# Attention: row sums by a column of ones, high halves on ScalarE, the sinks' values on GpSimd

## The chip, the cores and the metric

The kernel runs on one core of a Trainium2 chip. The metric is the device time of one execution in microseconds (us). A core has TensorE (matmuls, results in PSUM), VectorE, ScalarE, GpSimd, and SyncE, which here only issues transfers. Each engine runs its own instructions in its own order and waits on semaphores for the others.

## The reference

Three stages. Attention over batch 4, 8 heads, 768 positions, head width 64, with a window of 128 keys and 4 sink keys that every query sees; then a mixture of experts (top 1 of 8) over 3072 tokens; then a dense layer with x - tanh(x). The change is in the first stage alone, which computes

```
scores = scale * np.matmul(q, k.transpose(0, 1, 3, 2))
keep = is_sink | in_window                      # pos < n_sink, 0 <= rel < window
scores = np.where(keep, scores, -1000000000.0)
a = np.exp(scores - np.max(scores, axis=-1, keepdims=True))
a = a / (np.sum(a, axis=-1, keepdims=True) + 1e-09)
return np.matmul(a, v).astype(np.float32)
```

## The kernel before

Float32 operands are split into two float16 halves (high, and low = value - high), and a product is made of three matmuls: high x high, high x low, low x high.

*Units and slots.* Attention goes by units: a unit is a pair of heads of one batch, 16 in all. A unit has 6 query blocks of 128 positions (index i), each with two heads (h). The loop of stage_a runs over slots (102 of them); in a slot each step works on another block, with lags (LAG): scores of block s, mask and row maximum of s-1, exponentials of s-2, transposes and high halves of s-3, low halves of s-4, values of s-6. The engines' queues get the instructions in this written order, slot by slot:

```
ORDER = ["tr", "exp0", "exp1", "high", "low", "mask", "sc", "val"]
```

and at the end of each slot what was put down for it with later(), in the order in which it was put down, then the preparation of the next unit's values (prep_steps), then at_slot, which in the late slots loads and halves the first experts' weights (w.load on SyncE, w.prep on ScalarE and VectorE).

*Steps of a block.* mask_max (VectorE, L238) reads scores from PSUM, adds the mask and gives the row extreme; exps (ScalarE, L246) gives the exponentials and, by an accumulator that a second instruction reads, their row sums (sums); transposes (TensorE, L260); high (ScalarE, L266); low (VectorE, L272); values (TensorE, L283 to L285), which accumulates outputs in two PSUM banks, oa for blocks 0 to 3 and ob for 4 and 5.

*Sinks.* The weights of the 4 sink keys of the blocks that don't hold them in their window are gathered three times over into 48 columns (sink_weights), transposed after the values of blocks 2 and 4 (sink_turn), and split on VectorE: L296 casts the transposed weights to float16, L297 subtracts them where the low half is wanted. L288 multiplies them with VSK, the sinks' values. VSK comes from step vs of prep_steps: two VectorE instructions (L195 cast, L196 low half where wanted) and a GpSimd product with a block mask (L198).

*Normalization.* divisors (GpSimd, L302) adds 1e-9 to the sums, reciprocals (VectorE, L307), normal (VectorE, L317) multiplies the PSUM outputs with them: part 0 of 512 columns in the slot of block 4's values, part 1 of 256 columns in a later one. halves then splits the result in three parts of two blocks, on GpSimd (L181 high, L182 low). Ahead of each, SyncE issues a transfer (L327) that moves data only if a general path had been taken; it is not, but the instruction stands in SyncE's queue and its semaphore is waited for. turn (L339, L340 on SyncE) transposes the halves by DMA for the routing and copies them into token rows; SyncE's queue also holds the loads of q, k, v, of zeros and of weights. In the tail the last unit's halves are split by ScalarE (L330) and VectorE (L331).

Of the kernel before, what the change touches and what calls it, by code (L numbers as in the profile page):

```python
# [10 lines left out]
F32 = mybir.dt.float32  # L11
# [173 lines left out]
def prep_steps(nc, e, u):  # L185

    def v(h):
        if h == 0:
            u.V = e.tp.tile([128, 2, 2, NB, 64], F16, tag="V", name="V", bufs=3)
        f = lambda t: t.rearrange("p t d -> p (t d)")  # L190
        split2(nc, f(u.V[:, 0, h]), f(u.V[:, 1, h]), u.vf[:, S // 2 * h:S // 2 * h + S // 2])

    def vs():
        s16 = e.tp.tile([48, 64], F16, tag="s16", name="s16", bufs=2)
        nc.vector.tensor_copy(s16, u.sf)  # L195
        nc.vector.scalar_tensor_tensor(s16, s16, e.vlow, u.sf, op0=ALU.mult, op1=ALU.add)  # L196
        u.VSK = e.tp.tile([48, 4, 64], F16, tag="VSK", name="VSK", bufs=3)
        nc.gpsimd.tensor_tensor(u.VSK, s16.unsqueeze(1).to_broadcast([48, 4, 64]),  # L198
                                e.bmask.unsqueeze(2).to_broadcast([48, 4, 64]), op=ALU.mult)
    return [lambda: v(0), lambda: v(1), vs]  # L200
# [11 lines left out]
def scores(nc, e, u, i):  # L212

    if i == 0:
        u.mn, u.sums, u.rs = (e.sm.tile([128, 12], F32, tag=t, name=t, bufs=3) for t in ("mn", "sums", "rs"))
    if i % 2 == 0:
        u.P[i // 2] = e.pp.tile([128, 4, 2 * BR], F32, tag="P", name="P")
    c0 = c_first(i)
    n = 264 - c0
    k0 = max(i - 1, 0) * BR + (c0 if i else 4)  # L220
    kc, qc = slice(k0, k0 + n), slice(128 * i, 128 * i + 128)
    u.s[i] = []

# [51 lines left out]
def values(nc, e, u, i):  # L275
    if i in (0, 4):
        u.o.append(bank(e, ("oa", "ob")[i // 4]).rearrange("p (n d) -> p n d", d=64))
    p = u.PT.pop(i)
    bs = blocks(i)
    for j, (h, t) in enumerate(bs):  # L280
        o = u.o[i // 4][:, (2 * i + h) % 8]
        vh, vl = u.V[:, 0, h, t], u.V[:, 1, h, t]
        nc.tensor.matmul(o, lhsT=p[:, 0, j], rhs=vh, start=j == 0 and i in (0, 4), stop=False, skip_group_check=True)  # L283
        nc.tensor.matmul(o, lhsT=p[:, 0, j], rhs=vl, start=False, stop=False, skip_group_check=True)
        nc.tensor.matmul(o, lhsT=p[:, 1, j], rhs=vh, start=False, stop=False, skip_group_check=True)  # L285
    if i in (3, 5):
        o = u.o[0][:, 4:8] if i == 3 else u.o[1][:, 0:4]
        nc.tensor.matmul(o, lhsT=u.pks[i // 2 - 1], rhs=u.VSK, start=False, stop=True, skip_group_check=True)  # L288


def sink_turn(nc, e, u, part):
# [4 lines left out]
    nc.vector.tensor_copy(t, pk)  # L296
# [3 lines left out]
def divisors(nc, e, u, part):  # L300
    s = slice(*((0, 8), (8, 12))[part])
    nc.gpsimd.tensor_scalar(u.rs[:, s], u.sums[:, s], 1e-9, 1.0 / XS, op0=ALU.add, op1=ALU.mult)  # L302


def reciprocals(nc, e, u, part):
    s = slice(*((0, 8), (8, 12))[part])
    nc.vector.reciprocal(u.rs[:, s], u.rs[:, s])  # L307
# [12 lines left out]
def halves(nc, e, u, part, fast=False):  # L320

    a, z = ((0, 2), (2, 4), (4, 6))[part]
# [4 lines left out]
    nc.sync.dma_start(x[:, a:z], e.xg[r:r + 256, :].rearrange("(t p) c -> p t c", p=128), cond=e.genr, cond_hint=False)  # L327
# [198 lines left out]
def stage_a(tc, e, us, at_slot):  # L526

    nc = tc.nc
    with tc.tile_pool(name="tp", bufs=2) as e.tp, tc.tile_pool(name="pp", bufs=4) as e.pp, \
         tc.tile_pool(name="pw", bufs=4) as e.pw:  # L530
        units = [(b, hp) for b in range(B) for hp in range(H // 2)]
# [14 lines left out]
        def after(s, u):  # L546
# [10 lines left out]
            later(s + HALF2, lambda: halves(nc, e, u, 2))  # L557
# [16 lines left out]
        for s in range(last + 1):  # L574
# [856 lines left out]
```

## Time and profile before

| | |
|---|---|
| runs | 1053.58, 1054.61, 1057.43 us (median 1054.61) |
| profiled execution, its own time | 1058.27 us |
| its span, first to last instruction | 1056.6 us |
| mean granted TensorE clock | 0.968 of full speed |
| busy: TensorE / VectorE / ScalarE / GpSimd | 980.5 / 549.5 / 430.0 / 307.1 us |
| attention stage | about 14 to 223 us of the span |
| expert and dense stages | from about 223 us to the end |

Busy times are shares of the whole span; in the attention stage VectorE, ScalarE and GpSimd are much busier than later. The matmuls' ends are modelled, so a busy TensorE isn't TensorE at its peak.

### The profile page before, as it was taken

What the parts mean: (1) busy time and instruction counts of PE and PEld (TensorE: products, weight loads), DVE (VectorE), ACT (ScalarE), POOL (GpSimd) and SP (SyncE); (2) the same over time, 40 slices, a digit from 0 to 9 for tenths busy, and PEclk for the clock granted to TensorE, in tenths of its full rate; (3) what the DMA queues carried; (4) which work ended last, traced back from release to release, by engine and by line L of the source; (5) the groups of instructions that cost most, each with busy time, mean ns of one, the idle gap of its engine ahead of it and who ended that gap; (6) DMA issues with size and microseconds to landing.
All of it is one profiled execution on the core that took longest, in us unless ns stands there. A gap on an engine that the chain in (4) does not pass through costs nothing. (4 is left out here: it accounts for less than half of the span.)

```text
span 1056.6 us, 18953 instructions
## 1 busy us (share of the span) xinstructions
PE 980.5 (93%) x6883; PEld 546.3 (52%) x6883; DVE 549.5 (52%) x1283; ACT 430.0 (41%) x1210; POOL 307.1 (29%) x409
## 2 busy tenths in 40 slices
PE   6998987798887899999989999999999999999996
PEld 4665655575556466666644444444444444444442
DVE  5999998956325458473748987251151052053000
ACT  3787877743223344343425552351152152053000
POOL 4657766622000000000005552242142143143010
PEclk6999998799999999999999999999999999999998
DMA  4796789587729768693533316102002000000000
GB/s 139 223 260 198 211 184 289 167 177 239 183 80 221 205 187 249 133 271 92 152 84 80 100 46 175 40 1 60 20 1 50 30 1 11 24 8 10 21 31 21
DMA packets 144944, 123.45 MB, mean 117 GB/s; under 512 B 101488, under 2 KB 113776, under 8 KB 144816
## 3 DMA queue, kind: packets, MB, share of 16 engines
q1 hardware_dynamic: 130608, 85.70, 32.0%
q0 software_dynamic: 8160, 28.34, 8.3%
q10 hardware_dynamic: 6048, 7.76, 2.4%
q8 instruction: 72, 1.18, 0.4%
q14 instruction: 56, 0.46, 0.1%
HBM read 75.97 MB, written 23.79 MB: 94 GB/s over the span
## 5 line engine op out<-in xcount | busy, mean ns | idle before, releaser
L1089 DVE SCALAR_TENSOR_TENSOR w<-z 128x512 f32<-128x512 f32 x96 | 72.6, 756 | 215.1 <-ACT z L1087 211.6
L1077 POOL TENSOR_TENSOR gl<-w,gh 128x512 f16<-128x512 f32 x96 | 117.4, 1223 | 151.2 <-ACT gh L1076 150.9
L660 PE MATMUL s<-y,wi 128*128 128x512 f16 x384 | 145.5, 379 | 0.0
L661 PE MATMUL s<-y,wi 128*128 128x512 f16 x384 | 145.5, 379 | 0.0
L662 PE MATMUL s<-y,wi 128*128 128x512 f16 x384 | 145.5, 379 | 0.0
L660 PE MATMUL pt<-wo,gh 128*128 128x512 f16 x352 | 133.4, 379 | 0.0
L661 PE MATMUL pt<-wo,gh 128*128 128x512 f16 x352 | 133.4, 379 | 0.0
L662 PE MATMUL pt<-wo,gl 128*128 128x512 f16 x352 | 133.4, 379 | 0.0
L1087 ACT ACTIVATE z<-s 128x256 f32<-128x256 f32 x192 | 72.0, 380 | 107.8 <-PE s L662 107.2
L246 ACT ACTIVATE P<-P,mn 128x264 f32<-128x264 f32 (+1 forms) x192 | 93.5, 489 | 36.5 <-DVE mn L238 36.1
L728 POOL DMA_DIRECT2D w<-in_w_dram x30 | 16.2, 540 | 291.8 <-DVE f L741 206.0
L1109 ACT ACTIVATE ot<-pt 128x512 f32<-128x512 f32 x22 | 13.1, 597 | 194.2 <-PE pt L662 184.4
L260 PE MATMUL pt<-ident,P 128*128 128x128 f32 x352 | 62.8, 302 | 23.2 <-DVE PT L272 22.4
L228 PE MATMUL s<-kf,qf 64*128 64x264 f32 (+2 forms) x384 | 76.2, 460 | 7.1 <-DVE mn L238 4.6
L1110 POOL DMA_INDIRECT out_dram<-ot,idu x24 | 23.5, 979 | 195.7 <-ACT ot L1109 186.0
L660 PE MATMUL pt<-w,h 128*128 128x512 f16 x176 | 67.4, 383 | 6.6 <-ACT h L770 3.6
L1090 DVE SCALAR_TENSOR_TENSOR w<-s,w 128x512 f32<-128x512 f32 x96 | 66.4, 692 | 10.4 <-DVE w L1089 0.5
L238 DVE CUSTOM_DVE_ANT_0 P<-s,mask 128x264 f32<-128x264 f32 (+1 forms) x192 | 69.2, 395 | 0.3
L716 DVE SCALAR_TENSOR_TENSOR w<-stg,w 128x1024 f16<-128x1024 f32 x55 | 65.9, 1223 | 6.0 <-ACT w L710 4.1
L662 PE MATMUL pt<-w,h 128*128 128x512 f16 x176 | 67.5, 383 | 1.5 <-issue 1.5
L661 PE MATMUL pt<-w,h 128*128 128x512 f16 x176 | 67.3, 382 | 0.0
L1076 ACT CAST gh<-w 128x512 f16<-128x512 f32 x96 | 59.2, 617 | 11.8 <-DVE w L1090 11.7
(272 smaller groups left out, 2042.9 us busy)
## 6 DMA issues: line engine op xcount, KB each, us to landing
stg<-in_w_dram SPq DMA_DIRECT2D x64, 512.0 KB
w<-in_w_dram POOLq DMA_DIRECT2D x30, 512.0 KB, 4.6
kf<-in_kT_dram SPq DMA_DIRECT2D x16, 396.0 KB
qf<-in_qT_dram SPq DMA_DIRECT2D x16, 384.0 KB
vf<-in_vP_dram SPq DMA_DIRECT2D x16, 384.0 KB
xf<-xg SPq DMA_DIRECT2D x48, 128.0 KB
row<-hl SPq DMA_DIRECT2D x15, 384.0 KB
yc<-y ACTq DMA_DIRECT2D x10, 514.0 KB
```

What stands on the lines that cost most here:

```text
L228: nc.tensor.matmul(ps[:, c0:264], lhsT=u.qf[r, qc], rhs=u.kf[r, kc], start=True, stop=True, skip_group_check=True)
L238: nc.vector.tensor_tensor_reduce(out=u.P[i // 2][:, it % 4, c0:], in0=s[h][:, c0:264], in1=e.M[:, min(i, 2), c0:], op0=ALU.add, op1=ALU.mi ...
L246: nc.scalar.activation(p, p, AF.Exp, scale=-1.0, bias=u.mn[:, it:it + 1], accum_out=u.sums[:, it:it + 1])
L260: nc.tensor.transpose(ps[:, j], u.P[i // 2][:, it % 4, c0:c0 + 128], e.ident)
L660: nc.tensor.matmul(out, lhsT=lh, rhs=rh, start=start, stop=False)
L661: nc.tensor.matmul(out, lhsT=lh, rhs=rl, start=False, stop=False)
L662: nc.tensor.matmul(out, lhsT=ll, rhs=rh, start=False, stop=stop)
L716: nc.vector.scalar_tensor_tensor(lo, src, WS, hi, op0=ALU.mult, op1=ALU.subtract)
L1077: nc.gpsimd.tensor_tensor(gl[:, f], w, gh[:, f], op=ALU.subtract)
L1087: nc.scalar.activation(z[:, s], p[:, s], AF.Square, scale=1.0 / (YS * WIS), accum_out=e.zsum[:, n:n + 1])
L1089: nc.vector.scalar_tensor_tensor(w, z, -2.5, z, op0=ALU.add, op1=ALU.mult)
L1090: nc.vector.scalar_tensor_tensor(w, p, -2.0 / 15.0 * G2 / (YS * WIS), w, op0=ALU.mult, op1=ALU.mult)
```

## The change

Row sums no longer come from ScalarE's accumulator. The high halves of the values get a 65th column of ones (V, in three fixed buffers whose ones are written once), so that the matmuls with the high halves of the values also add the weights up into column 64 of each output block; VSK gets such a column too. Output blocks are 65 columns wide, and oa and ob hold three query blocks each. normal adds 1e-9 to column 64, takes the reciprocal and multiplies, all on VectorE, for three blocks at a time; divisors and reciprocals go. halves has two parts of three blocks; the high half is a ScalarE copy for every unit. In sink_turn the high half is a ScalarE copy too. Step vs is on GpSimd alone (three small instructions and the product with the block mask). The sink matmul of blocks 2 and 3 becomes two, as these lie in different banks.

```diff
 def v(h):
         if h == 0:
-            u.V = e.tp.tile([128, 2, 2, NB, 64], F16, tag="V", name="V", bufs=3)
-        f = lambda t: t.rearrange("p t d -> p (t d)")
-        split2(nc, f(u.V[:, 0, h]), f(u.V[:, 1, h]), u.vf[:, S // 2 * h:S // 2 * h + S // 2])
+            e.V.append(e.V.pop(0))
+            u.V = e.V[0]
+        split2(nc, u.V[:, 0, h, :, 0:64], u.V[:, 1, h, :, 0:64],
+               u.vf[:, S // 2 * h:S // 2 * h + S // 2].rearrange("p (t d) -> p t d", d=64))
 def vs():
-        s16 = e.tp.tile([48, 64], F16, tag="s16", name="s16", bufs=2)
-        nc.vector.tensor_copy(s16, u.sf)
-        nc.vector.scalar_tensor_tensor(s16, s16, e.vlow, u.sf, op0=ALU.mult, op1=ALU.add)
-        u.VSK = e.tp.tile([48, 4, 64], F16, tag="VSK", name="VSK", bufs=3)
-        nc.gpsimd.tensor_tensor(u.VSK, s16.unsqueeze(1).to_broadcast([48, 4, 64]),
-                                e.bmask.unsqueeze(2).to_broadcast([48, 4, 64]), op=ALU.mult)
+        e.s16.append(e.s16.pop(0))
+        s16 = e.s16[0]
+        t = s16[:, 0:64]
+        nc.gpsimd.tensor_scalar(t, u.sf, 1.0, 1.0, op0=ALU.mult, op1=ALU.mult)
+        nc.gpsimd.tensor_tensor(t, t, e.vlow.to_broadcast([48, 64]), op=ALU.mult)
+        nc.gpsimd.tensor_tensor(t, u.sf, t, op=ALU.add)
+        u.VSK = e.tp.tile([48, 4, 65], F16, tag="VSK", name="VSK", bufs=3)
+        nc.gpsimd.tensor_tensor(u.VSK, s16.unsqueeze(1).to_broadcast([48, 4, 65]),
+                                e.bmask.unsqueeze(2).to_broadcast([48, 4, 65]), op=ALU.mult)
 def exps(nc, e, u, i, h):
-    nc.scalar.activation(p, p, AF.Exp, scale=-1.0, bias=u.mn[:, it:it + 1], accum_out=u.sums[:, it:it + 1])
+    nc.scalar.activation(p, p, AF.Exp, scale=-1.0, bias=u.mn[:, it:it + 1])
 def values(nc, e, u, i):
-    if i in (0, 4):
-        u.o.append(bank(e, ("oa", "ob")[i // 4]).rearrange("p (n d) -> p n d", d=64))
+    if i in (0, 3):
+        u.o.append(bank(e, ("oa", "ob")[i // 3])[:, 0:390].rearrange("p (n d) -> p n d", d=65))
...
-        vh, vl = u.V[:, 0, h, t], u.V[:, 1, h, t]
+        vh, vl = u.V[:, 0, h, t], u.V[:, 1, h, t, 0:64]
...
     if i in (3, 5):
-        o = u.o[0][:, 4:8] if i == 3 else u.o[1][:, 0:4]
-        nc.tensor.matmul(o, lhsT=u.pks[i // 2 - 1], rhs=u.VSK, start=False, stop=True, skip_group_check=True)
+        pks = u.pks[i // 2 - 1]
+        for o, v in ((u.o[0][:, 4:6], u.VSK[:, 0:2]), (u.o[1][:, 0:2], u.VSK[:, 2:4])) if i == 3 else \
+                ((u.o[1][:, 2:6], u.VSK),):
+            nc.tensor.matmul(o, lhsT=pks, rhs=v, start=False, stop=True, skip_group_check=True)
 def sink_turn(nc, e, u, part):
-    nc.vector.tensor_copy(t, pk)
+    nc.scalar.copy(t, pk)
     nc.vector.scalar_tensor_tensor(t, t, e.plow, pk, op0=ALU.mult, op1=ALU.add)
-def divisors(nc, e, u, part): ...
-def reciprocals(nc, e, u, part): ...
 def normal(nc, e, u, part):
-    r4 = u.rs[:, s].rearrange("p (i h) -> p i h", h=2).unsqueeze(3).to_broadcast([128, z - a, 2, 64])
-    o = u.o[part][:, 0:2 * (z - a)].rearrange("p (i h) d -> p i h d", h=2)
-    nc.vector.tensor_tensor(u.x[:, a:z], o, r4, op=ALU.mult)
+    o = u.o[part]
+    r = u.rs[:, 6 * part:6 * part + 6]
+    nc.vector.tensor_scalar(r, o[:, :, 64], 1e-9, 1.0 / XS, op0=ALU.add, op1=ALU.mult)
+    nc.vector.reciprocal(r, r)
+    nc.vector.tensor_tensor(u.x[:, 3 * part:3 * part + 3].rearrange("p i h d -> p (i h) d"), o[:, :, 0:64],
+                            r.unsqueeze(2).to_broadcast([128, 6, 64]), op=ALU.mult)
 def halves(nc, e, u, part, fast=False):
-    a, z = ((0, 2), (2, 4), (4, 6))[part]
+    a, z = ((0, 3), (3, 6))[part]
...
-    if fast:
-        nc.scalar.copy(hi, x[:, a:z])
-        (nc.vector if fast else nc.gpsimd).tensor_tensor(lo, x[:, a:z], hi, op=ALU.subtract)
-    else:
-        split2(nc, hi, lo, x[:, a:z])
+    nc.scalar.copy(hi, x[:, a:z])
+    (nc.vector if fast else nc.gpsimd).tensor_tensor(lo, x[:, a:z], hi, op=ALU.subtract)
 def stage_a(tc, e, us, at_slot):
+        e.V = [e.tp.tile([128, 2, 2, NB, 65], F16, name=f"V{i}", bufs=1) for i in range(3)]
+        e.s16 = [e.tp.tile([48, 65], F16, name=f"s16{i}", bufs=1) for i in range(2)]
+        for t in e.V:
+            nc.gpsimd.memset(t[:, 0, :, :, 64:65], 1.0)
+        for t in e.s16:
+            nc.gpsimd.memset(t[:, 64:65], 1.0)
+            nc.gpsimd.memset(t[32:48, 64:65], 0.0)
...
-                            divisors(nc, e, g[0], g[1] // 2 - 1)
...
-                        if i5 in RECIP:
-                            later(s, lambda u=u, p=RECIP.index(i5): reciprocals(nc, e, u, p))
                         if i5 == 3:
                             later(s + 1, lambda u=u: normal(nc, e, u, 0), lambda u=u: halves(nc, e, u, 0))
-                            later(s + HALF1, lambda u=u: halves(nc, e, u, 1))
```

The last part of halves is number 1 now, at the same slot as number 2 before; the tail calls it too.

## Rows read from the trace of the kernel before

**Rows 1.** Busy time of each engine in two stretches of the attention stage.

```profile
core 0: us, PE busy (x) PEld busy (x) DVE busy (x) ACT busy (x) POOL busy (x), PEclk, DMA share, GB/s
...
120.00:132.00 12.00, 11.47 (x147) 7.64 (x146) 11.55 (x46) 10.34 (x38) 8.17 (x16) 1.00 0.66 189
...
204.00:216.00 12.00, 11.09 (x93) 7.18 (x93) 8.55 (x30) 6.45 (x21) 7.75 (x13) 0.57 0.49 134
```

**Rows 2.** Timeline, VectorE, a quiet unit: start, length, line [idle before, releaser].

```profile
118.24 0.41 DVE L317 TENSOR_TENSOR xf<-ob,rs 128x256 f32<-128x256 f32 x1
...
121.55 0.28 DVE L296 CAST pks<-s 48x128 f16<-48x128 f32 x1 [0.15 <-PE s L294]
...
129.00 0.41 DVE L317 TENSOR_TENSOR xf<-ob,rs 128x256 f32<-128x256 f32 x1
```

**Rows 3.** Timeline, VectorE, the slot of block 4 of another unit.

```profile
114.40 0.68 DVE L317 TENSOR_TENSOR xf<-oa,rs 128x512 f32<-128x512 f32 x1
115.00 0.27 DVE L296 CAST pks<-s 48x128 f16<-48x128 f32 x1
115.31 0.34 DVE L297 SCALAR_TENSOR_TENSOR pks<-pks,plow,s 48x128 f16<-48x128 f16 x1
```

**Rows 4.** Groups by form, VectorE, 20 to 400: count | busy us, mean ns | idle.

```profile
L196 DVE SCALAR_TENSOR_TENSOR s<-s,vlow,sf 48x64 f16<-48x64 f16 x14 | 5.9, 418 | 0.5
L195 DVE CAST s<-sf 48x64 f16<-48x64 f32 x14 | 5.6, 400 | 0.0
...
L307 DVE RECIPROCAL rs<-rs 128x8 f32<-128x8 f32 x16 | 3.0, 190 | 0.0
```

**Rows 5.** Timeline, VectorE, a small tensor_scalar behind the stage.

```profile
242.55 0.17 DVE L410 TENSOR_SCALAR gs<-gs 128x6 f32<-128x6 f32 x1
```

**Rows 6.** Groups by form, ScalarE, 20 to 400.

```profile
L246 ACT ACTIVATION_READ_ACCUMULATOR P<-P,mn 128x1 f32 x187 | 35.3, 189 | 0.0
...
L266 ACT CAST PT<-pt 128x256 f16<-128x256 f32 x15 | 5.3, 355 | 1.1 <-PE pt L260 1.1
```

**Rows 7.** Timeline, GpSimd, the cast behind the product of rows 3.

```profile
115.32 0.40 POOL L181 TENSOR_SCALAR hl<-xf 128x256 f16<-128x256 f32 x1 [1.76 <-DVE pks L296]
```

**Rows 8.** Timeline, ScalarE, the last unit's halves in the tail.

```profile
227.40 0.41 ACT L330 CAST hl<-xf 128x256 f16<-128x256 f32 x1 [7.18 <-DMA row<-hl]
```

**Rows 9.** Timeline, TensorE, two successive matmuls of 64 columns.

```profile
115.75 0.19 PE L284 MATMUL ob<-V,PT 128*128 128x64 f16 x1
115.78 0.19 PE L285 MATMUL ob<-V,PT 128*128 128x64 f16 x1
```

**Rows 10.** Timeline, SyncE's queue, the unit at 151.

```profile
153.69 0.42 SPq L327 DMA_DIRECT2D xf<-xg  x2
...
159.07 0.33 SPq L170 DMA_DIRECT2D sf<-in_vS_dram  x1
...
164.35 0.09 SPq L327 DMA_DIRECT2D xf<-xg  x1
```

**Rows 11.** Timeline, VectorE, the two products of that unit.

```profile
151.43 0.67 DVE L317 TENSOR_TENSOR xf<-oa,rs 128x512 f32<-128x512 f32 x1
...
155.43 0.41 DVE L317 TENSOR_TENSOR xf<-ob,rs 128x256 f32<-128x256 f32 x1
```

**Rows 12.** Timeline, ScalarE, at the end of that unit.

```profile
156.41 0.58 ACT L266 CAST PT<-pt 128x512 f16<-128x512 f32 x1
...
160.81 1.06 ACT L710 ACTIVATE w<-stg 128x1024 f16<-128x1024 f32 x1 [1.63 <-DMA stg<-in_w_dram]
```

**Rows 13.** Timeline, SyncE's queue, the tail.

```profile
221.26 2.90 SPq L339 DMA_TRANSPOSE xT<-hl  x1
...
225.18 0.08 SPq L327 DMA_DIRECT2D xf<-xg  x1
```

**Rows 14.** Timeline, VectorE, the last unit's first product.

```profile
221.62 0.69 DVE L317 TENSOR_TENSOR xf<-oa,rs 128x512 f32<-128x512 f32 x1
```

**Rows 15.** Timeline, TensorE, the last sink matmul.

```profile
222.94 0.28 PE L288 MATMUL ob<-VSK,pks 48*128 48x256 f16 x1 [0.86 <-DVE pks L297]
```

More of the change, by code (lines that the diff above doesn't have):

```diff
@@ L214, in scores @@
     if i == 0:
-        u.mn, u.sums, u.rs = (e.sm.tile([128, 12], F32, tag=t, name=t, bufs=3) for t in ("mn", "sums", "rs"))
+        u.mn, u.rs = (e.sm.tile([128, 12], F32, tag=t, name=t, bufs=3) for t in ("mn", "rs"))
     if i % 2 == 0:
@@ L280, in values @@
     for j, (h, t) in enumerate(bs):
-        o = u.o[i // 4][:, (2 * i + h) % 8]
-        vh, vl = u.V[:, 0, h, t], u.V[:, 1, h, t]
-        nc.tensor.matmul(o, lhsT=p[:, 0, j], rhs=vh, start=j == 0 and i in (0, 4), stop=False, skip_group_check=True)
-        nc.tensor.matmul(o, lhsT=p[:, 0, j], rhs=vl, start=False, stop=False, skip_group_check=True)
+        o = u.o[i // 3][:, (2 * i + h) % 6]
+        vh, vl = u.V[:, 0, h, t], u.V[:, 1, h, t, 0:64]
+        nc.tensor.matmul(o, lhsT=p[:, 0, j], rhs=vh, start=j == 0 and i in (0, 3), stop=False, skip_group_check=True)
+        nc.tensor.matmul(o[:, 0:64], lhsT=p[:, 0, j], rhs=vl, start=False, stop=False, skip_group_check=True)
         nc.tensor.matmul(o, lhsT=p[:, 1, j], rhs=vh, start=False, stop=False, skip_group_check=True)
     if i in (3, 5):
-        o = u.o[0][:, 4:8] if i == 3 else u.o[1][:, 0:4]
-        nc.tensor.matmul(o, lhsT=u.pks[i // 2 - 1], rhs=u.VSK, start=False, stop=True, skip_group_check=True)
+        pks = u.pks[i // 2 - 1]
+        for o, v in ((u.o[0][:, 4:6], u.VSK[:, 0:2]), (u.o[1][:, 0:2], u.VSK[:, 2:4])) if i == 3 else \
+                ((u.o[1][:, 2:6], u.VSK),):
+            nc.tensor.matmul(o, lhsT=pks, rhs=v, start=False, stop=True, skip_group_check=True)
 def sink_turn(nc, e, u, part):
@@ L295, in sink_turn @@
     t = u.pks[part] = e.sm.tile([48, 128], F16, tag="pks", name="pks")
-    nc.vector.tensor_copy(t, pk)
+    nc.scalar.copy(t, pk)
     nc.vector.scalar_tensor_tensor(t, t, e.plow, pk, op0=ALU.mult, op1=ALU.add)
[L300 to L307, printed above, removed]
 def normal(nc, e, u, part):
-    a, z = ((0, 4), (4, 6))[part]
     if part == 0:
         u.x = e.rx.tile([128, NB, 2, 64], F32, tag="xf", name="xf")
-    s = slice(2 * a, 2 * z)
-    r4 = u.rs[:, s].rearrange("p (i h) -> p i h", h=2).unsqueeze(3).to_broadcast([128, z - a, 2, 64])
-    o = u.o[part][:, 0:2 * (z - a)].rearrange("p (i h) d -> p i h d", h=2)
-    nc.vector.tensor_tensor(u.x[:, a:z], o, r4, op=ALU.mult)
+    o = u.o[part]
[4 more added lines that the diff above has]
+                            r.unsqueeze(2).to_broadcast([128, 6, 64]), op=ALU.mult)
 def halves(nc, e, u, part, fast=False):
-    a, z = ((0, 2), (2, 4), (4, 6))[part]
+    a, z = ((0, 3), (3, 6))[part]
     x = u.x.rearrange("p i h d -> p i (h d)")
@@ L326, in halves @@
     r = (u.b * H // 2 + u.hp) * S + 128 * a
-    nc.sync.dma_start(x[:, a:z], e.xg[r:r + 256, :].rearrange("(t p) c -> p t c", p=128), cond=e.genr, cond_hint=False)
+    nc.sync.dma_start(x[:, a:z], e.xg[r:r + 384, :].rearrange("(t p) c -> p t c", p=128), cond=e.genr, cond_hint=False)
     hi, lo = u.hl[:, a:z, 0], u.hl[:, a:z, 1]
-    if fast:
-        nc.scalar.copy(hi, x[:, a:z])
-        (nc.vector if fast else nc.gpsimd).tensor_tensor(lo, x[:, a:z], hi, op=ALU.subtract)
-    else:
-        split2(nc, hi, lo, x[:, a:z])
+    nc.scalar.copy(hi, x[:, a:z])
+    (nc.vector if fast else nc.gpsimd).tensor_tensor(lo, x[:, a:z], hi, op=ALU.subtract)
 def turn(nc, e, u, row, queue):
@@ L499 @@
 PICK = 6
-RECIP = [3, 5]
 SCAT = [5, 5, 4]
 SINKS = [2, 4]
-HALF1, HALF2, TURN = 2, 2, 3
+HALF2, TURN = 2, 3
 WARM = 22
@@ L552, in after @@
                 es, sc = expert_steps(nc, e, u.b, row)
-                tail = [lambda: normal(nc, e, u, 1), lambda: halves(nc, e, u, 2, True),
+                tail = [lambda: normal(nc, e, u, 1), lambda: halves(nc, e, u, 1, True),
                         lambda: turn(nc, e, u, row, nc.scalar), lambda: logits(nc, e, u)]
@@ L556, in after @@
             later(s + 1, lambda: normal(nc, e, u, 1))
-            later(s + HALF2, lambda: halves(nc, e, u, 2))
+            later(s + HALF2, lambda: halves(nc, e, u, 1))
             later(s + TURN, lambda: turn(nc, e, u, row, nc.sync))
```

## The prediction

> **What bounds the kernel now.** I read the page's busy shares first (TensorE 93%), then the stretches of 12 us through the attention stage, because a share over 1056 us mixes stages. In a quiet stretch of attention VectorE is busy 11.55 of 12 us, ScalarE 10.34, GpSimd 8.17, at full TensorE clock [rows 1]. From the end of attention on, TensorE runs nearly without a gap, so what attention gains or loses is passed on to the end almost one for one. Nothing of the change lies behind attention but one copy and one subtraction in its tail.
>
> The timeline of VectorE gives the rhythm: its last product of one unit (a pair of heads) starts at 118.24, that of the next at 129.00: 10.76 us, with little but a wait of 0.15 in between [rows 2]. Units with routing steps take longer, also on VectorE. So VectorE's instruction stream, in its order, is what sets the pace, and the question is what the change does to that stream: work taken off it, and waits put into it.
>
> **The change part by part, on VectorE, for one unit.**
>
> *Products and sums.* Before: a product of 512 columns, 0.60 from its start to that of the next instruction, 114.40 to 115.00 [rows 3]; a product of 256 columns, 0.41 long [rows 2], taken as 0.34 by the same overlap of 0.07; two reciprocals, 0.19 for 8 columns [rows 4], half overlapped, 0.1 each. Together 1.14. After, twice: an addition over 6 columns, then its reciprocal, then the product of 384 columns, each needing the one before. The addition is like a 128x6 tensor_scalar of 0.17 [rows 5], the reciprocal is 0.17; a dependent successor starts some 0.03 after the end, as 115.00 plus 0.27 to 115.31 shows [rows 3]; the product lies between 0.41 and 0.68, taken 0.54, less 0.07. That is 0.20 + 0.20 + 0.47, say 0.88, twice 1.76. So +0.62.
>
> *The sinks' values* leave VectorE: 0.40 + 0.42 by their means [rows 4], so -0.8.
>
> *The high half of the sinks' weights* leaves VectorE: 0.31 twice, 115.00 to 115.31 [rows 3], so -0.62.
>
> Work alone is thus 0.62 - 0.8 - 0.62 = -0.8 us a unit. The Trainium skill says in Perfetto Trace Analysis, Optimizing Scalar/DVE Operations, that with a saturated VectorE handing work to ScalarE or GpSimd may pay. By that alone the sum would be 15 units at -0.8, or -12 us; by the waits worked out next it is a loss.
>
> **The waits.** The low half (L297) stays on VectorE and now needs ScalarE's copy, which ends sink_turn's hand-over. Part 0 (in the slot of query block 2): the transpose ends when VectorE is about to arrive, it waited 0.15 for it [rows 2]; now a ScalarE copy of 128 columns stands between. A ScalarE cast of 256 columns from PSUM is 0.355 [rows 6], so some 0.25, and 0.06 for two hand-overs: +0.31.
>
> Part 1 (block 4's slot) is the crux. In program order that slot has normal(0), halves(0), sink_turn(1). Before, halves ran on GpSimd, and VectorE went straight from the product to L296 and L297 [rows 3]. Now halves issues on ScalarE a copy that waits for the product and for SyncE's conditional transfer, and the sink copy is queued behind it on ScalarE. The delay from the product to the reader behind that transfer is seen on GpSimd: the product ends at 114.40 + 0.68 = 115.08, the cast starts at 115.32 [rows 3, 7]: 0.24. ScalarE's cast of 256 columns from SBUF took 0.41 [rows 8]; 384 lie between that and 0.61, I take 0.5, with some 0.45 until the next starts. Then the sink copy, 0.25, and 0.03. VectorE, which has nothing else before L297, stands 0.24 + 0.45 + 0.25 + 0.03 = 0.97, and 0.07 more as its overlap is lost: +1.04. Behind L297 stand the next slot's low half and mask, and behind these ScalarE's exponentials: the delay is not caught up.
>
> Sum for a unit: -0.8 + 0.31 + 1.04 = +0.55. I take 0.5 over 15 units (the last is counted below): **+7.5 us**. Bounds: -12 us if neither wait is seen, +20 if also each addition with its reciprocal costs 0.8, as L195 with L196 did.
>
> *Hidden parts.* ScalarE loses 12 reads of its accumulator, 0.19 each at most [rows 6], and gains two casts of 0.5 and two copies of 0.25; that is at best -0.8, and it has slack of 1.7 in 12 [rows 1]. GpSimd loses three casts of 0.40 [rows 7] and gets three small ones for the sinks, no longer than these: nothing, and its idle 3.8 us [rows 1] cover it. If its writes in rows of 65 cost double, they still fit. The matmuls with 65 instead of 64 columns follow each other at 0.03 us [rows 9]: 704 of them, a 64th more, 0.3 us, hidden; the upper bound, one more such step for each, is 21 us of TensorE spread over attention, which only touches the range. The seven fills at the start are on GpSimd before the first values are used, nothing; at most 0.40 each, +2.8. One transfer less a unit moves no data: nothing.
>
> **Where SyncE is late.** Its queue now stands in front of ScalarE's, twice a unit. Mostly SyncE is ready before the product is [rows 7]. Not in the unit at 151: there the transfer of the first part was issued at 153.69, though the product had ended at 152.10 [rows 10, 11]: +1.6. The last transfer came at 164.35, with its product done by 155.84; SyncE was held by loads before it, one of them at 159.07 [rows 10, 11]. GpSimd took that without harm. ScalarE would be at that copy after its cast at 156.41 + 0.58 = 156.99 [rows 12], 159.1 with the delays of this unit, and would be free at 164.35 + 0.2 + 0.45 = 165.0: 5.9 us, with the weight cast, the next exponentials and so VectorE behind it. Of that, 1.63 were a wait of ScalarE for a weight load before [rows 12], which is over by then: +4.3. Together **+6** (0 if the slower pace gives SyncE its time, 10 if nothing is absorbed).
>
> **The tail.** The last unit's product starts at 221.62, but SyncE is in the turn's transpose from 221.26 on and issues the transfer at 225.18 [rows 13, 14]. Only GpSimd waited. Now ScalarE's copy, the sink copy and L297 follow on it: 225.18 + 0.2 + 0.45 + 0.25 + 0.03 + 0.34 + 0.05 = 226.5 for the last sink matmul, which stood at 222.94 [rows 15]. The first expert matmuls are behind it in TensorE's queue: **+3.5** (at least 1, by the chain without SyncE's lateness). The longer copies for the rows of the last unit, some 0.3 us, fall beside TensorE's expert work: nothing.
>
> **Sum.** 7.5 + 6 + 3.5 = 17 us. The profiled execution took 1058.27 by its own clock (span 1056.6), 3.7 above the median of the runs, 1054.61. Against its own time 1075.3, as a median of runs 1071.6: I say **1071**.
>
> **Rivals.**
>
> *Faster: the offload pays.* If the ScalarE copies are in time (the cast of halves done within some 0.2 us of the product, or SyncE's hand-over shorter), VectorE keeps its -0.8: 1054.6 - 12 = 1043. For it: VectorE is at 96% in a quiet stretch [rows 1]. Against it: the 0.24 [rows 7] repeats wherever GpSimd had been idle before the product. It decides where the two waits of a unit together fall below 0.8. Chance 0.14. The sentence of the Trainium skill's Perfetto Trace Analysis on handing work to ScalarE speaks for this one.
>
> *No change.* The waits just eat the gain (0.8 in a unit), and the late transfers [rows 10, 13] are met by the later pace: within 5.3 us of 1054.6. Chance 0.10.
>
> *Much slower: the clock.* In the stretch from 204 the granted clock was 0.57, mostly the lower of its two levels, 1.2 GHz, and TensorE got through 93 matmuls in 11.09 busy us, where a quiet stretch has 147 in 11.47 [rows 1]. At that rate a unit takes 10.76 x 147/93 = 17 us, 6 more. Waits of several us on TensorE, as ScalarE's at 159, could bring more such stretches: two or three units, 12 to 18 us on top, 1083 to 1089. Or 65 columns cost a step each, to the same effect. Chance 0.10.
>
> **How the numbers follow.** The forecast, 1060 to 1084, has 0.66. With the clock's rival slower by over 0.5% (5.3 us, about what a measurement of this kernel can tell from no change) has 0.76, within 0.5% 0.10, faster 0.14. The range must hold the forecast, no change and a little of either side: 1048 to 1085 leaves out most of the faster case and half of the clock's.
>
> **What would show it.** Right: L195, L196, L296, L302 gone from VectorE and GpSimd; before L297 an idle time of about 1 us in block 4's slot, ended by ScalarE's copy, and one of 0.3 to 0.45 in block 2's; ScalarE's cast of halves preceded by waits for the transfer, one of several us near 160 and one near the tail; quiet units of about 11.3 us; the first expert matmul some 13 to 18 us later than at 223. Wrong: L297 without idle time before it; quiet units below 10.76; a first expert matmul before 223.

## The result, and the profile after

The changed kernel took 1062.74 us (median of 9 runs, 1059.45 to 1066.06), the kernel before 1055.29 us beside it (9 runs, 1052.19 to 1060.55): a ratio of 1.0066, interval 1.0042 to 1.0089, some 7 us slower where the forecast said 16. The profiled execution took 1060.96 us.

First the steady part. A quiet unit is one of the short ones, with little work beside attention. Busy time of each engine over two of them (from the last product of one unit to that of the next), changed kernel:

```profile
core 0: us, PE busy (x) PEld busy (x) DVE busy (x) ACT busy (x) POOL busy (x), PEclk, DMA share, GB/s
40.83:52.15 11.32, 10.46 (x132) 7.07 (x130) 9.76 (x39) 9.24 (x25) 5.96 (x10) 1.00 1.09 255
52.15:63.44 11.29, 10.46 (x132) 7.08 (x130) 9.77 (x40) 9.24 (x25) 5.97 (x10) 1.00 1.11 278
```

A quiet unit lasts 11.3 us where it lasted 10.76 [rows 2], and VectorE is busy for 9.76 us of it. The same view of the kernel before, the unit of [rows 2]:

```profile
118.24:129.00 10.76, 10.23 (x130) 6.92 (x128) 10.31 (x42) 9.10 (x33) 7.01 (x14) 1.00 0.67 184
```

So 0.55 us of VectorE's work went and 1.09 us of waits came. VectorE's timeline shows where they stand, in block 2's slot and in block 4's:

```profile
55.64 0.34 DVE L304 SCALAR_TENSOR_TENSOR pks<-pks,plow,s 48x128 f16<-48x128 f16 x1 [0.45 <-ACT pks L303]
...
58.42 0.19 DVE L313 RECIPROCAL rs<-rs 128x6 f32<-128x6 f32 x1
58.71 0.56 DVE L314 TENSOR_TENSOR xf<-oa,rs 128x384 f32<-128x384 f32 x1
60.14 0.34 DVE L304 SCALAR_TENSOR_TENSOR pks<-pks,plow,s 48x128 f16<-48x128 f16 x1 [0.88 <-ACT pks L303]
```

and ScalarE's timeline shows why the second is long: its cast of the halves stands idle until the product is out, the sink copy is queued behind it, then the exponentials:

```profile
59.44 0.51 ACT L327 CAST hl<-xf 128x384 f16<-128x384 f32 x1 [1.09 <-DVE xf L314]
59.85 0.25 ACT L303 CAST pks<-s 48x128 f16<-48x128 f32 x1
60.01 0.92 ACT L250 ACTIVATE P<-P,mn 128x264 f32<-128x264 f32 x2
```

The groups by form, 20 to 400 us (count | busy us, mean ns | idle before), give the durations of the new instructions:

```profile
L304 DVE SCALAR_TENSOR_TENSOR pks<-pks,plow,s 48x128 f16<-48x128 f16 x32 | 10.8, 337 | 29.0 <-ACT pks L303 29.0
L314 DVE TENSOR_TENSOR xf<-ob,rs 128x384 f32<-128x384 f32 x16 | 8.9, 557 | 0.5
L313 DVE RECIPROCAL rs<-rs 128x6 f32<-128x6 f32 x32 | 6.1, 191 | 1.1
L312 DVE TENSOR_SCALAR rs<-oa 128x6 f32<-128x6 f32 x16 | 2.4, 150 | 0.0
L327 ACT CAST hl<-xf 128x384 f16<-128x384 f32 x32 | 16.4, 512 | 32.8 <-DMA xf<-xg 23.7 <-DVE xf L314 5.6 <-DMA row<-hl 3.6
L303 ACT CAST pks<-s 48x128 f16<-48x128 f32 x32 | 8.2, 257 | 12.8 <-PE s L301 12.8
L200 POOL TENSOR_TENSOR s<-sf,s 48x64 f16<-48x64 f32 x15 | 5.6, 375 | 1.2
```

The late waits are there too. Timelines of ScalarE, VectorE, SyncE's queue and TensorE, one unit near 150 and the tail:

```profile
151.94 0.08 SPq L325 DMA_DIRECT2D xf<-xg  x1
152.16 0.51 ACT L327 CAST hl<-xf 128x384 f16<-128x384 f32 x1 [3.86 <-DMA xf<-xg]
152.86 0.34 DVE L304 SCALAR_TENSOR_TENSOR pks<-pks,plow,s 48x128 f16<-48x128 f16 x1 [3.40 <-ACT pks L303]
...
159.33 0.51 ACT L327 CAST hl<-xf 128x384 f16<-128x384 f32 x1 [1.99 <-DMA xf<-xg]
...
227.48 0.89 SPq L335 DMA_DIRECT2D row<-hl  x1
228.69 0.08 SPq L325 DMA_DIRECT2D xf<-xg  x1
228.85 0.51 ACT L327 CAST hl<-xf 128x384 f16<-128x384 f32 x1 [3.69 <-DMA xf<-xg]
229.56 0.34 DVE L304 SCALAR_TENSOR_TENSOR pks<-pks,plow,s 48x128 f16<-48x128 f16 x1 [2.48 <-ACT pks L303]
229.95 0.28 PE L295 MATMUL ob<-VSK,pks 48*128 48x260 f16 x1 [3.13 <-DVE pks L304]
```

SyncE issues the conditional transfer at 151.94 and 228.69, ScalarE's cast follows 0.2 us later, and one after the other VectorE and TensorE. The last sink matmul comes at 229.95 us, 7.0 later than before [rows 15].

What no step of the forecast held is at the start. The first unit's last product starts at 29.59 us; before, at 36.44. Timelines of VectorE and ScalarE, kernel before:

```profile
12.25 0.47 DVE L195 CAST s<-sf 48x64 f16<-48x64 f32 x1 [2.56 <-DMA sf<-in_vS_dram]
12.76 0.99 DVE L196 SCALAR_TENSOR_TENSOR s<-s,vlow,sf 48x64 f16<-48x64 f16 x1
13.68 0.27 DVE L238 CUSTOM_DVE_ANT_0 P<-s,mask 128x128 f32<-128x128 f32 x1
...
16.23 0.40 DVE L195 CAST s<-sf 48x64 f16<-48x64 f32 x1
16.66 1.00 DVE L196 SCALAR_TENSOR_TENSOR s<-s,vlow,sf 48x64 f16<-48x64 f16 x1
...
36.44 0.41 DVE L317 TENSOR_TENSOR xf<-ob,rs 128x256 f32<-128x256 f32 x1
...
14.04 1.28 ACT L246 ACT_TABLE_LOAD   x1 [14.04 <-DVE mn L238]
15.34 0.40 ACT L246 ACTIVATE P<-P,mn 128x128 f32<-128x128 f32 x1
```

and after:

```profile
9.69 0.29 DVE L242 CUSTOM_DVE_ANT_0 P<-s,mask 128x128 f32<-128x128 f32 x1
...
29.59 0.56 DVE L314 TENSOR_TENSOR xf<-ob,rs 128x384 f32<-128x384 f32 x1
...
8.25 1.28 ACT L250 ACT_TABLE_LOAD   x1 [8.25 <-ACTq L1293]
```

Before, the first unit's cast of the sinks' values stood at the head of VectorE's queue for a load, with the first mask behind it and ScalarE's table load of 1.28 us behind the mask. After, the mask starts at 9.69 and the table is loaded before it.

### The profile page after: what moved, and what is told of

The parts are those of the page before. It is cut to its first block, busy times and chain, and to the rows that moved or that the text cites. A ratio compares the mean times of both kernels' runs of the same rounds, so it can differ in the third digit from the quotient of the medians.

```text
span 1059.3 us, 18769 instructions
## 1 busy us (share of the span) xinstructions
PE 981.2 (93%) x6899; PEld 548.6 (52%) x6899; DVE 537.9 (51%) x1251; ACT 431.0 (41%) x1081; POOL 290.5 (27%) x369
## 5 line engine op out<-in xcount | busy, mean ns | idle before, releaser
L250 ACT ACTIVATE P<-P,mn 128x264 f32<-128x264 f32 (+1 forms) x192 | 84.6, 489 | 11.7 <-DVE mn L242 11.6
L1073 ACT CAST gh<-w 128x512 f16<-128x512 f32 x96 | 59.2, 617 | 11.4 <-DVE w L1087 11.3
```

## The experiments

The table has all kernels by the start of the last product (VectorE, L314 or the line that answers to it): of the first unit, then the sum of the next nine gaps between units, of the last six (those with the weights' loads in SyncE's queue), the last unit's; then a quiet unit, the median, and the ratio to the kernel before run beside it.

| kernel | first | nine gaps | six gaps | last | quiet unit | median us | ratio |
|---|---|---|---|---|---|---|---|
| before | 36.44 | 106.11 | 80.70 | 223.25 | 10.76 | | |
| changed | 29.59 | 109.67 | 91.43 | 230.69 | 11.3 | 1062.7 | 1.0066 (1.0042, 1.0089) |
| vs_first_vector | 34.61 | 108.50 | 90.72 | 233.83 | 11.3 | 1067.4 | 1.0107 (1.0064, 1.0150) |
| vs_two_vector | 37.76 | 109.58 | 91.02 | 238.36 | 11.3 | 1071.8 | 1.0149 (1.0117, 1.0181) |
| vs_alone | 28.52 | 103.23 | 77.86 | 209.61 | 10.15 | 1042.0 | 0.9860 (0.9820, 0.9901) |
| vs_first_alone | 38.33 | 105.38 | 81.34 | 225.05 | 10.8 | 1060.3 | 1.0025 (0.9997, 1.0053) |
| vs_first_later | 37.42 | 105.98 | 80.78 | 224.18 | 10.8 | 1057.3 | 1.0005 (0.9974, 1.0036) |
| vs_first_two | 29.92 | 104.78 | 78.97 | 213.67 | 10.85 | 1046.9 | 0.9922 (0.9895, 0.9949) |
| vs_two_later | 30.85 | 104.12 | 79.70 | 214.67 | 10.8 | 1050.2 | 0.9955 (0.9936, 0.9974) |
| order | 29.92 | 104.90 | 88.18 | 223.00 | 11.13 | 1057.8 | 1.0004 (0.9976, 1.0032) |
| sink_vector | 29.82 | 106.40 | 89.40 | 225.62 | 11.15 | 1060.7 | 1.0004 (0.9977, 1.0032) |
| halves_late | 29.05 | 102.63 | 88.58 | 220.26 | 10.30 | 1057.7 | 0.9992 (0.9961, 1.0024) |
| halves_gpsimd | 29.64 | 98.82 | 79.58 | 208.04 | 10.30 | 1046.7 | 0.9897 (0.9857, 0.9936) |
| halves_gpsimd_sink_vector | 29.80 | 103.52 | 80.06 | 213.38 | 10.65 | 1045.4 | 0.9881 (0.9836, 0.9926) |
| halves_gpsimd_sink_split | 28.09 | 98.19 | 80.45 | 206.73 | 10.16 | 1040.6 | 0.9854 (0.9821, 0.9887) |
| sink_split | 29.54 | 102.02 | 77.19 | 208.75 | 10.01 | 1043.4 | 0.9849 (0.9808, 0.9889) |

The medians of the kernel before beside them were 1055.3 to 1058.5 us. Across all fifteen, the shift of the last product and that of the time (the ratio less 1, times the median of before) agree within 4.3 us, and differ by 1.6 us on average: what attention gains or loses is passed on nearly one for one.

**The start.** vs_first_vector: the changed kernel, the first unit's sinks' values on VectorE.

```diff
+        if (u.b, u.hp) == (0, 0):
+            nc.vector.tensor_copy(t, u.sf)
+            nc.vector.scalar_tensor_tensor(t, t, e.vlow, u.sf, op0=ALU.mult, op1=ALU.add)
+        else:
             nc.gpsimd.tensor_scalar(t, u.sf, 1.0, 1.0, op0=ALU.mult, op1=ALU.mult)
...
```

> The changed kernel, with the first unit's sinks' values computed on VectorE as before (two instructions), all other units' on GpSimd. Theory (the first unit's cast waits on VectorE for a load and the first mask stands behind it; that wait is what the change removed at the start): the first mask moves from 9.7 back to about 13.7 us, the first exponential from 10.0 to about 14.0, the whole attention stage 4 us later, 1062.7 + 4 = 1067. Rival (the early start comes from elsewhere, or what it gains is lost again to later loads): the first mask late, but the end of attention within 1 us of the changed kernel's, 1063.

The first mask went back to 13.72 and the first product to 34.61, 5.0 of the 6.85 us. So the start hangs on the sinks' values, and the time, 1067.4 us, is the one named. The table load went back behind the mask as well (14.08), which I had not expected.

vs_alone: the kernel before, only the sinks' values on GpSimd, in all units.

```diff
-        nc.vector.tensor_copy(s16, u.sf)
-        nc.vector.scalar_tensor_tensor(s16, s16, e.vlow, u.sf, op0=ALU.mult, op1=ALU.add)
+        nc.gpsimd.tensor_scalar(s16, u.sf, 1.0, 1.0, op0=ALU.mult, op1=ALU.mult)
+        nc.gpsimd.tensor_tensor(s16, s16, e.vlow.to_broadcast([48, 64]), op=ALU.mult)
+        nc.gpsimd.tensor_tensor(s16, u.sf, s16, op=ALU.add)
```

> The kernel before, with nothing changed but the sinks' values: three small GpSimd instructions in place of the two of VectorE. Theory: first mask at 9.7 instead of 13.7 (-4), and 0.6 to 0.8 us of VectorE's work gone in each of 15 units (-10): about 1041 against 1055, quiet units of 10.1 in place of 10.76. Rival (VectorE's work in a unit is not what sets the pace): quiet units stay at 10.7, -4 at most, 1051.

1042.0 us: this part of the change alone is worth 14.8 us, 7.9 of the 13.6 by which the last product moved at the start, the rest in the gaps. The quiet unit is 0.6 us shorter for 0.57 less of VectorE's work (10.31 before, 9.74 after).

vs_first_alone: the same three lines in the kernel before, for the first unit only (`if (u.b, u.hp) == (0, 0)`); vs_first_later: no other engine, but VectorE's two instructions issued later.

```diff
-        for f in prep_steps(nc, e, us[0]):
-            f()
+        v0, v1, vs0 = prep_steps(nc, e, us[0])
+        v0()
+        v1()
+        later(3, vs0)
```

> The kernel before, with the sinks' values on GpSimd in the first of the sixteen units only. Theory (in the kernel before, the first cast of the sinks' values holds VectorE's queue for its load, and the first mask and the first exponential stand behind it): the first unit's last product starts near 29.5 instead of 36.4 us, the gaps between the later ones stay as before (186.8 us from the first to the last), and the time falls by about 7 us, to 1050. Rival (what is gained at the start is taken back by the loads that the later units wait for): the gaps grow by about as much, and the time is 1055 or above.

> The kernel before, with the sinks' values of the first unit left on VectorE but issued at the end of the fourth slot instead of ahead of the first mask; no engine does other work than before. Theory (it is the place in VectorE's queue, not the engine, that the start hangs on): the first mask starts near 9.7 us and the first unit's last product near 30 us, the time about 1050 us. Rival (the start needs VectorE's two operations gone, or GpSimd doing them): the first mask starts after 13 us or the first product after 34 us, and the time is 1055 or above.

Both theories fell at the first product: the first mask did start at 9.7 us in both, but the first product came at 38.33 and 37.42, later than before, and neither kernel gained time. VectorE's timeline in vs_first_alone, and in it ScalarE's:

```profile
18.01 0.42 DVE L200 CAST s<-sf 48x64 f16<-48x64 f32 x1 [6.38 <-DMA sf<-in_vS_dram]
...
20.73 0.52 ACT L251 ACTIVATE P<-P,mn 128x264 f32<-128x264 f32 x1 [8.06 <-DVE mn L243]
```

The second unit's cast, which stood at 16.23 without a wait in the kernel before, takes the first one's place: VectorE, sooner there, waits 6.38 us for that unit's load. Two waits stood in line, and taking away the first uncovers the second. That the first product comes even later than before has a further source: the same load, issued at 11.26 us in the kernel before, had landed there by 16.23, and was waited for until 18.01 here and 17.20 in vs_first_later; why it landed later was not tried. That made a new theory, for three kernels: vs_first_two (the condition is `u.b == 0 and u.hp < 2` instead), vs_two_vector (the changed kernel, both units' values back on VectorE by the same condition), and vs_two_later:

```diff
+        later(6, vs0)
...
                     wait += prep_steps(nc, e, us[n + 1])
+                    if n == 0:
+                        later(7, wait.pop())
```

> The kernel before, with the sinks' values of the first two units on GpSimd and those of the other fourteen on VectorE as before. Theory (the first two casts, each behind its load in VectorE's queue, are the whole of the late start): the first unit's last product starts between 28.5 and 30 us instead of 36.4, the gaps stay near 186.8 us from the first to the last, and the time is about 1049 to 1051 us. Rival (a third wait takes their place, as the second took the first's): the first product starts after 34 us and the time is 1055 us or above.

> The changed kernel, with the sinks' values of the first two units back on VectorE and the other fourteen on GpSimd. Theory: the early start is gone whole, the first unit's last product starts near 36.5 to 37 us instead of 29.6, and the time is about 1069 to 1070 us, which is where the forecast of 1071 lay. Rival (the changed kernel's start has another source as well): the first product stays below 35 us, where it was with the first unit's alone on VectorE (34.6), and the time at 1067 or below.

> The kernel before, with the sinks' values of the first two units left on VectorE but issued six and seven slots into the loop, when their loads have landed; no engine does other work than before. Theory (it is the place in VectorE's queue, not the engine): the first product starts near 30 to 31 us (two operations of 0.3 to 1.0 us each per unit still stand in the queue), the time is about 1050 to 1052 us. Rival (it is VectorE's work itself): the first product starts after 34 us, the time is 1055 us or above.

In all three the first product moved as the theory said. Two sizes lie outside what it named: vs_first_two, at 1046.9 us, is 2 us faster, as its gaps shrank a little too, and vs_two_vector has its first product at 37.76, 0.8 us later, and takes 1071.8 us, 1.8 more. VectorE's timeline in vs_two_vector has both casts again, each behind a wait, though the first of them (as in vs_first_vector) ends with GpSimd's cast of the values and not with the load:

```profile
12.71 0.92 DVE L199 CAST s<-sf 48x64 f16<-48x64 f32 x1 [3.02 <-POOL V L181]
...
17.23 0.40 DVE L199 CAST s<-sf 48x64 f16<-48x64 f32 x1 [0.62 <-DMA sf<-in_vS_dram]
```

With them the changed kernel takes 1071.75 us. vs_two_later shows that most of it is the place in the queue and not the engine: VectorE does all the work of before, and the first product starts at 30.85.

**The copies on ScalarE.** order: the changed kernel, but the slot of block 4 does the product, then the sinks, then the halves.

```diff
+                        if i5 == 4:
+                            later(s, lambda u=u: normal(nc, e, u, 0))
                         if i5 in SINKS:
                             later(s, lambda u=u, p=SINKS.index(i5): sink_turn(nc, e, u, p))
-                        if i5 == 3:
-                            later(s + 1, lambda u=u: normal(nc, e, u, 0), lambda u=u: halves(nc, e, u, 0))
+                        if i5 == 4:
+                            later(s, lambda u=u: halves(nc, e, u, 0))
```

> The changed kernel, with the same instructions in another order in block 4's slot: normal, sink_turn, halves in place of normal, halves, sink_turn, so that ScalarE's copy of the sinks' weights is no longer queued behind its copy of the halves. Theory (VectorE's wait before L304 in that slot, about 1.0 us, lengthens every unit): the wait falls to under 0.2, quiet units from 11.3 to 10.3, and the last sink matmul no longer waits for SyncE (-2.5): 1062.7 - 14 - 2.5, about 1046. Rival (the wait only takes the place of others, ScalarE being as late anyway): quiet units stay above 11, time within 4 us of 1062.7.

VectorE's wait in block 4's slot went, but the quiet unit fell by 0.17 us alone, neither to the 10.3 of the theory nor with the time of its rival. ScalarE's and VectorE's timelines in that kernel:

```profile
58.73 0.26 ACT L303 CAST pks<-s 48x128 f16<-48x128 f32 x1 [0.37 <-PE s L301]
59.45 0.51 ACT L327 CAST hl<-xf 128x384 f16<-128x384 f32 x1 [0.46 <-DMA xf<-xg]
...
59.20 0.33 DVE L304 SCALAR_TENSOR_TENSOR pks<-pks,plow,s 48x128 f16<-48x128 f16 x1
59.46 0.68 DVE L276 TENSOR_TENSOR PT<-pt,PT 128x512 f16<-128x512 f32 x1
...
61.57 0.69 DVE L276 TENSOR_TENSOR PT<-pt,PT 128x512 f16<-128x512 f32 x1 [0.73 <-ACT PT L270]
```

ScalarE still stands before its cast of the halves, and VectorE pays for it at 61.57, at the next low half of the weights but one. So in a quiet unit VectorE's wait at L304 was where the delay showed, not what it was. The time fell all the same, from 1062.7 to 1057.8 us: the nine gaps are 4.77 us shorter, more than quiet units explain, as two longer units fell too (from 13.57 to 12.53 us each), and the last gap fell from 8.23 to 5.67, as the last sink matmul no longer stands behind SyncE's transfer.

sink_vector puts the sink copy back on VectorE (`nc.vector.tensor_copy(t, pk)`), halves_late the cast one slot behind its product:

```diff
-                            later(s + 1, lambda u=u: normal(nc, e, u, 0), lambda u=u: halves(nc, e, u, 0))
+                            later(s + 1, lambda u=u: normal(nc, e, u, 0))
+                            later(s + 2, lambda u=u: halves(nc, e, u, 0))
```

and halves_gpsimd puts the cast back on GpSimd for all units but the last:

```diff
-    nc.scalar.copy(hi, x[:, a:z])
-    (nc.vector if fast else nc.gpsimd).tensor_tensor(lo, x[:, a:z], hi, op=ALU.subtract)
+    if fast:
+        nc.scalar.copy(hi, x[:, a:z])
+        nc.vector.tensor_tensor(lo, x[:, a:z], hi, op=ALU.subtract)
+    else:
+        split2(nc, hi, lo, x[:, a:z])
```

> The changed kernel with the high half of the sinks' weights copied by VectorE again (two copies of 0.28 us a unit), all else as changed. Theory (VectorE's waits for ScalarE's copy are what a unit loses): the waits of 0.45 us in block 2's slot and 0.9 us in block 4's go, 0.56 us of work comes, so a quiet unit falls from 11.3 to about 10.5 us and the time to about 1050 us. Rival (ScalarE, which copies the halves of the outputs and waits for SyncE's transfer ahead of it, sets the unit): ScalarE still waits for the product and the transfer, so the unit falls only by ScalarE's own 0.52 us of copies or less, to 10.8 or above, and the time is 1056 or above.

> The changed kernel with the first part's transfer and halves issued one slot later than its product, instead of in the same slot; ScalarE's work stays as it is, its wait for the product and for SyncE goes. Theory A (it is the wait of ScalarE's queue for product and transfer that costs): the unit falls to about 10.5 us and the time to about 1050 us, though the later transfers in the second half of attention may still cost some. Theory B (ScalarE's own work sets the unit, 1.02 us of copies of the halves): the unit stays at 11.0 us or above and the time at 1058 us or above.

> The changed kernel, with the high halves of the outputs on GpSimd again (two parts of three blocks), so that no instruction of ScalarE waits for SyncE's conditional transfers; the sinks' weights stay on ScalarE. Theory (two costs: the 1.0 us wait in each unit, and the late transfers in front of ScalarE near 150 to 160 and in the tail): quiet units 10.3, no wait of several us on VectorE near 150 to 160, first expert matmul 2 to 3 us sooner after the last product: about 1044, a little below the order experiment. Rival (GpSimd becomes late with 0.5 us more for each part, or the late transfers cost nothing): the same time as the order experiment or more.

In sink_vector the quiet unit stays at 11.15 though both waits of VectorE are gone, as the rival said: ScalarE stands before its cast as long as in the changed kernel.

```profile
59.43 0.51 ACT L327 CAST hl<-xf 128x384 f16<-128x384 f32 x1 [1.08 <-DVE xf L314]
```

In halves_late, with the same work on ScalarE, the quiet unit falls to 10.30, the same as with the cast on GpSimd. The busy times of a quiet unit, halves_late and then halves_gpsimd:

```profile
49.77:60.07 10.30, 10.18 (x131) 6.87 (x130) 9.66 (x39) 9.21 (x25) 5.98 (x10) 1.00 1.13 266
```

```profile
50.18:60.48 10.30, 10.18 (x131) 6.94 (x130) 9.65 (x39) 8.56 (x23) 5.51 (x11) 1.00 1.12 246
```

So in a quiet unit it is ScalarE's wait that costs, about 1.0 us, and not its work. But the time of halves_late is 1057.7, not 1050: its last six gaps are 88.58 us, against 79.58 with the cast on GpSimd. There ScalarE still waits for SyncE's late transfers, in one case for 4.7 us, as its waits from 132 to 240 us show (us in total, times, longest):

```profile
ACT hl L327 <- DMA xf<-xg: 8.6, 4, 4.7
```

Only with the cast on GpSimd, which can be late without harm, do both parts go: 10.85 us in the nine gaps and 11.85 in the six. The time, 1046.7 us, is 2.7 above the one named.

**What is left, and the better versions.** halves_gpsimd_sink_vector has both edits above; sink_split is vs_alone with the sink copy on ScalarE and VectorE's low half put behind the next slot's low half; halves_gpsimd_sink_split is halves_gpsimd with the same deferral.

```diff
     nc.scalar.copy(t, pk)
-    nc.vector.scalar_tensor_tensor(t, t, e.plow, pk, op0=ALU.mult, op1=ALU.add)
+    e.behind_low.append(lambda: nc.vector.scalar_tensor_tensor(t, t, e.plow, pk, op0=ALU.mult, op1=ALU.add))
...
+                if k == "low":
+                    while e.behind_low:
+                        e.behind_low.pop(0)()
```

> The changed kernel with both copies off ScalarE: the halves of the outputs on GpSimd and the high half of the sinks' weights on VectorE, as before. What is left of the change is the sinks' values on GpSimd, the sums by the column of ones and the outputs in two equal parts. Theory (VectorE is the bound once ScalarE is early): two copies of 0.28 us come and two waits of about 0.45 us go, so the unit is 10.2 to 10.4 us, and the time is 1045 to 1049 us, the same as with the copies on ScalarE. Against the kernel before with the sinks' values alone on GpSimd (10.14 us, 1042 us) this is the price of the sums by column: about 0.1 to 0.2 us a unit for the two adds on VectorE. Rival (the column spares ScalarE twelve reads of an accumulator a unit, and that counts): 10.0 us or less and 1040 us or less.

> The kernel before with the sinks' values on GpSimd, and with the high half of the sinks' weights by ScalarE, but VectorE's low half issued in the next slot, behind the low half of that slot's weights, so that it need not wait for ScalarE. Sums by the exponentials' accumulators, outputs as before. Theory (VectorE is the bound, and the offload pays where nothing waits): 0.56 us less of VectorE a unit, against 0.3 us or so that comes as ScalarE's share: the unit falls from 10.14 to 9.7 to 9.9 us and the time from 1042 to 1035 to 1038 us. Rival (ScalarE with its accumulator reads is as full as VectorE): 10.1 us or more and 1041 us or more.

> The changed kernel with the halves of the outputs on GpSimd as before, and VectorE's low half of the sinks' weights issued one slot later, so that it does not stand waiting for ScalarE's copy. Theory (VectorE is the bound and its two waits of 0.45 us a unit count): the quiet unit falls from 10.3 to about 9.6 us, the first nine gaps from 98.8 to about 93 us, and the time from 1046.7 to about 1040 us. Rival (another engine is as full; TensorE is busy for 10.2 of the 10.3 us by its modelled ends): 10.1 us or more a unit, and 1043 us or above.

halves_gpsimd_sink_vector took the time I named, but with a quiet unit of 10.65, outside what either theory gave. The other two missed on the unit: 10.01 and 10.16 us, not below 9.9. sink_split missed on the time as well, 1043.4 us; the time of halves_gpsimd_sink_split, 1040.6 us, is the theory's all the same, in part by a first product 1.55 us earlier than that of halves_gpsimd, which no theory held. The quiet units of sink_split, vs_alone and halves_gpsimd_sink_split have TensorE busy from end to end (by its modelled ends):

```profile
39.47:49.48 10.01, 10.01 (x130) 6.81 (x128) 9.32 (x40) 9.43 (x35) 7.35 (x15) 1.00 1.20 259
```

```profile
38.40:48.55 10.15, 10.15 (x130) 6.88 (x128) 9.74 (x42) 9.10 (x33) 7.17 (x15) 1.00 0.96 266
```

```profile
48.40:58.56 10.16, 10.16 (x131) 6.92 (x133) 9.72 (x40) 8.53 (x23) 4.98 (x10) 1.00 1.14 235
```

VectorE is busy for 96% of the last two, as it was in the kernel before [rows 1], and for 93% of sink_split's, where 0.42 us less of its work than in vs_alone gave a unit only 0.14 us shorter. Sparing VectorE more than the sinks' values thus buys little here. That TensorE is what holds the unit at 10.0 to 10.2 us is suggested by these rows and not shown: VectorE is nearly as full in two of them, and neither was tried by itself. vs_alone, sink_split and halves_gpsimd_sink_split, 1.4 to 1.5% below the kernel before, can't be told apart; vs_alone gets there with the three GpSimd instructions alone.

## Why the prediction was half right

*The steady unit.* Right in its sum: 11.3 us as written, +0.54 against 10.76, for a forecast of +0.55. That it fits so closely is luck: 0.55 us of work went, not 0.8, and 1.09 us of waits came, not 1.35, and the two misses cancel. The first nine gaps grew by 3.56 us, where nine times 0.5 is 4.5. The single pieces hold: waits of 0.45 and 0.88 to 0.96 us at L304 (forecast 0.46, from 0.15 and 0.31, and 1.04), a product of 0.557, a sink copy of 0.257, a cast of 0.512 us (0.54, 0.25 and 0.5). The cause was put one step too near, at VectorE: order and sink_vector show that ScalarE's wait costs a quiet unit whether VectorE stands at L304 or not.

*SyncE late, and the tail.* Right within 2 us in the sum: forecast 3 (six gaps at 0.5), 6 and 3.5, together 12.5; the last six gaps grew by 10.73. The places are those named, but the two sizes near 150 came the other way about: ScalarE waited 3.86 us at 152.16 and 1.99 at 159.33, and the two gaps grew by 4.25 and 1.44, where the forecast had 1.6 and 4.3 with 0.5 each for the unit. That the sum comes near is luck. The last gap grew by 2.79, and order, which takes the last sink matmul away from SyncE, gives back 2.56 of it. halves_gpsimd, at 79.58, shows that ScalarE's copies of the halves are all of the 10.73.

*The step that failed* is "The sinks' values leave VectorE: 0.40 + 0.42 by their means, so -0.8". I took two groups by their mean busy time, as work of a repeated unit, and multiplied by 15. Even for a repeated unit that was too much, 0.6 us by vs_alone; but the large miss is at the start. In the first two units these instructions also stand at the head of VectorE's queue when their loads have hardly landed, with the first masks behind them (in the kernel before a wait of 2.56 us for the first, and 6.38 for the second once the first is gone). Of the start the sum holds only the fills, at nothing; the view that I read began at 20 us, behind it. Measured, the start is worth -6.85 us: 17.0 forecast at the last sink matmul less 6.85 is 10.1, and 7.0 was measured there. With the start given back, vs_two_vector takes 1071.75 us, 1.49% or 15.7 us above the kernel before: the forecast of 1071 was near that of the changed kernel without its early start. That it meets it to within 1 us is luck in part: vs_two_vector starts 1.3 us later than the kernel before, and its gaps grew by 13.8 us, not 17.

*The rivals.* None was the start. "The offload pays" is right for the sinks' values, which went from VectorE to GpSimd. The Trainium skill, in Perfetto Trace Analysis, Optimizing Scalar/DVE Operations, says that with a saturated VectorE offloading to ScalarE or even GpSimd may make sense, and that to GpSimd it might not help, as the two share a read port of SBUF. Here it did help: GpSimd's share saved 14.8 us (vs_alone), over half of it at the start. The sink copy that went from VectorE to ScalarE cost some 6.5 us queued behind ScalarE's cast of the halves (1.0066 against 1.0004 in sink_vector), and with that cast on GpSimd nothing that can be told from noise (0.9897 against 0.9881). The cast of the halves itself cost some 18 us on ScalarE (1.0066 against 0.9897), but it came from GpSimd, so it spared VectorE nothing. The clock's rival did not come in the time: over the first 240 us the mean granted clock was 0.90 in both kernels. From 132 to 168 us it was 0.82 against 0.89, around the late transfers; what that cost was not separated.

*Passing on.* "Almost one for one" holds over the fifteen kernels, within the 4.3 us. In the one pair of profiles only 2.7 us of span are left of 7.4 at the last product, less than the scatter of single runs, 6.6 and 8.4 us.

## What to carry to other kernels

Before an instruction is priced by its group's mean, look at its first occurrences: where it waits for a load at the head of an in-order queue, everything behind it waits too, and its removal can be worth that wait, once; then see which instruction would be the next to wait, because vs_first_alone moved the first mask by 4 us and gained nothing. As for moved work, an engine whose queue feeds others should not be given an instruction that waits for a late transfer; an engine that nobody waits for can hold it, and a slot's delay is the second best cure. A wait that a profile puts on one engine can be the image of another's: moving it, as order did, tells which.

## What the runs showed of the hardware that I had not expected

ScalarE's table load of 1.28 us stood at 14.04 us, right behind the first mask, where VectorE's cast of the first unit's sinks' values stood ahead of that mask, and at 8.2 to 8.3 us, before the mask, where it did not (vs_alone, vs_first_later and the changed kernel). In vs_first_vector and vs_two_vector it was at 14.08 and 14.42. So the place of a table load changed with an edit to another engine's queue; why was not tried.

The second unit's sinks' values, loaded by an instruction that SyncE issued at 11.04 us, let VectorE start only at 18.01 (vs_first_alone): some 7 us for a transfer of 12 KB, while the core's transfers kept their engines 0.92 busy from 12 to 15 us. In the kernel before it was issued at 11.26 and was there by 16.23, at most 5 us.
